# Second chunk's query transposes moved from TensorE to VectorE, with a new load form, in an mLSTM and gelu kernel

## The chip, the cores and the metric

The kernel runs on one core of one Trainium2 chip. The metric is the device time of one execution in microseconds (us). The kernel before takes 467.68 us, the median of three runs (467.54 to 468.31).

The core has a matrix engine (TensorE, PE in the profile), a vector engine (VectorE, DVE), a scalar engine (ScalarE, ACT), GpSimd (POOL), and SyncE (SP), which here only issues DMA transfers. Each engine executes its own instructions in the order in which the program gives them, and waits at an instruction until what that instruction needs is there.

## The reference

An mLSTM cell runs over 768 tokens for 4 batches of 8 heads with 40 numbers each. Per head it keeps a 40 x 40 state C, a vector n and a running maximum m:

```python
m_new = max(f[t] + m, i[t])
C = exp(f[t] + m - m_new) * C + exp(i[t] - m_new) * outer(v[t], k[t])
n = exp(f[t] + m - m_new) * n + exp(i[t] - m_new) * k[t]
y[t] = sigmoid(o[t]) * (C @ q[t]) / max(abs(n @ q[t]), 1)
```

The heads of a token are put side by side (320 numbers), and a feed-forward block follows for the 3072 tokens: `h = x @ w_in` (2048 wide), `g = h * sigmoid(1.702 h)`, `out = g @ w_out` (320 wide). Everything is float32.

## The kernel before, in words

**Chunks.** The 768 tokens are cut into six chunks of 128, numbered w = 0 to 5. A chunk's attention is done in matrix form: scores of its keys and queries, weighted by the gates, plus what the state carries in. Then its 512 tokens (4 batches x 128) go through the feed-forward block. In the main loop (line 888) iteration w does the feed-forward block of chunk w, and interleaves the attention of chunk w + 1 into it. The order is written out by hand: each engine gets its instructions in the order of the Python calls.

**Keys and queries as columns.** The scores need keys and queries with the head's numbers along the partitions, `kT` and `qT`, one tile per batch. There are two ways to them:
- `transposes` (line 372) for chunks 0 and 1. `load` (line 110) brings tokens onto partitions, heads and numbers along the row, in packets of 160 bytes (one head of one token). TensorE transposes two heads at a time into a PSUM tile, four for keys and four for queries per batch, and a copy per tile brings the result to SBUF: keys by ScalarE, queries of chunk 1 by VectorE (line 382).
- `block_transposes` (line 385) for chunks 2 to 5. `load_squares` (line 102) brings rows of four consecutive tokens, in packets of 640 bytes; every row is loaded twice, the second time shifted by 32 numbers and on other partitions. VectorE then transposes blocks of 32 x 32 straight from SBUF to SBUF, one instruction for the keys or the queries of a batch (even n: keys, odd n: queries, n // 2 the batch).

The tile `q_sq` holds the queries in both forms (`q_st` is a view of it). The keys of chunk 1 lie in `k_1`, a view of `t_sb`.

**The weights.** The float32 weights come as raw words and are brought into another form on the chip, in 20 pieces of 512 columns: pieces 0 to 9 are `w_in` (2 and 7 the "rests", the last 64 rows), 10 to 19 are `w_out`. `fetch(n)` issues the load on SyncE; `convert(n)` is two ScalarE instructions and then four on VectorE (lines 256 to 265). The pieces are converted while the feed-forward block of chunk 0 is running, just ahead of their use.

**Iteration 0.** Its first half runs `up` (line 603) for pairs of hidden blocks j = 0 to 7, two pairs per call. A pair takes full matmuls over `w_in_sb` (line 615) and the rest matmuls over 64 rows (line 621): two matmuls of 512 columns, on the two halves of the array. Then ScalarE applies the gelu. Around the calls stand conversions (the list `converted`, line 874), the gates of chunk 1 (j = 3), its value load, and, at j = 4 to 7, `transposes(1, j - 4)`. The pieces are converted in the order 3, 4, then 5 behind the first pair; 6 ahead of pair 2, then 7 and 8; the gates; 9 and 10 ahead of pair 4, then 11 and 12; 13 ahead of pair 6, then 14, 15 and 16.

The second half begins with `columns_turn(1)`, a VectorE transpose of the gate columns. Then `down` (line 744) runs in 16 blocks of four hidden row blocks each; piece 17 is converted ahead of the first, 18 and 19 ahead of the fifth and sixth. Behind certain blocks stand the steps of chunk 1's attention: ScalarE's exponentials of the columns, `scale` on GpSimd, `carry` (the state update, TensorE, line 591), `scores`, `values`.

**Loads around the edit.** SyncE's queue runs in order. After the gate loads of chunk 1 (`load_gates(1)`, line 857), `load(1, "kq")` (line 858) issues three key loads and one query load; the next in the queue are the fetches of pieces 10 to 17. A new DMA also waits until an earlier one that used the same one of eight semaphores has landed.

Of the kernel before, what the change touches and what calls it, by code (L numbers as in the profile page):

```python
# [26 lines left out]
def kernel(  # L27
# [19 lines left out]
    NF = DFF // 128  # L47
    D1 = D + 1
    DP = 64
    W = B * L  # L50
# [44 lines left out]
    def k_of(w):  # L95
        return (k_0, k_1)[w] if w < 2 else k_st[:, 0:BH * D].rearrange("s (h d) -> s h d", d=D)
# [5 lines left out]
    def load_squares(w, what):  # L102
        for dst, src in [((k_sq, k), (q_sq, q))["kq".index(c)] for c in what]:
            x = src[:, :, w * L:(w + 1) * L, :].rearrange("b (p two) (r c) d -> two r (b p) (c d)", two=2, c=4)
            for i in range(2):
                for n in range(2):
                    r, at = slice(i * 64 + n * 32, i * 64 + n * 32 + 32), (1 - n) * 32
                    nc.sync.dma_start(out=dst[r, at:at + BH // 2 * 4 * D].rearrange("r (j x) -> r j x", x=4 * D), in_=x[i])

    def load(w, what, bs=slice(0, B)):  # L110
        hs = slice(bs.start * H, bs.stop * H)
        for c in what:
            if c == "o" and w not in eo:
                eo[w] = ld.tile([L, BH, D], FP, tag="eo", bufs=1, name="eo")
            dst, src = {"k": (k_of(w), k), "q": (q_st, q), "v": (v_st, v), "o": (eo.get(w), o_gate)}[c]
            if w and c in "kv":
                for i, t, r in ((0, slice(0, L), slice(0, L)), (1, slice(0, HL), slice(HL, L)),
                                (1, slice(HL, L), slice(0, HL))):
                    x = src[:, :, w * L + t.start:w * L + t.stop, :].rearrange("b (p two) s d -> two s (b p) d", two=2)
                    nc.sync.dma_start(out=dst[r, i::2, 0:D], in_=x[i])  # L120
                continue
            nc.sync.dma_start(out=dst[:, hs, 0:D],
                              in_=src[bs, :, w * L:(w + 1) * L, :].rearrange("b h s d -> s (b h) d"))
# [226 lines left out]
    def columns_turn(w):  # L350
        c = cols[w] = gate.tile([L, 4 * BH], FP, name="cols")
        V.transpose(out=c[:, 0:3 * BH].rearrange("p (k h) -> p k h", h=BH),
                    in_=raw[w][:, 0:3 * BH].rearrange("p (k t) -> p k t", t=32))
# [16 lines left out]
        A.activation(out=eo[w], in_=eo[w], func=AF.Tanh, scale=0.5)  # L370

    def transposes(w, b, between=None):
        for dst, name in ((kT, "kT"), (qT, "qT")):
            dst[w, b] = work.tile([128, NP, L], FP, tag=name, bufs=4, name=name)
        pt = banks("p_t")
        for x, src in enumerate((k_of(w), q_st)):
            if x and between:
                between()
            for p in range(NP):
                h = b * H + 2 * p  # L380
                T.transpose(pt[:, x, p * L:(p + 1) * L], src[:, h:h + 2, :].rearrange("p a b -> p (a b)"), ident)  # L381
        for x, (dst, copy) in enumerate(((kT, A.copy), (qT, V.tensor_copy if w else A.copy))):
            copy(out=dst[w, b].rearrange("r j t -> r (j t)"), in_=pt[:, x, :])

    def block_transposes(w, n):
        b, (to, name, src) = n // 2, ((kT, "kT", k_sq), (qT, "qT", q_sq))[n % 2]
        at, n = 32 + b * NP * 4 * D, NP * 4 * D
        to[w, b] = work.tile([128, NP, L], FP, tag=name, bufs=4, name=name)
        V.transpose(out=to[w, b].rearrange("d j (r c) -> d j c r", c=4),
                    in_=src[:, at:at + n].rearrange("r (j c d) -> r j c d", c=4, d=D)[:, :, :, 0:32])  # L390
# [212 lines left out]
    def up(w, j, between):  # L603


        x = xT[w].rearrange("p c b t -> p c (b t)")
        ph = {}

        def full(j, first, cs=range(2)):
            for c in cs:  # L610
                for i in range(2):
                    f = 2 * j + i
                    for n in range(2):
                        t = slice(n * W // 2, (n + 1) * W // 2)
                        T.matmul(ph[j][i][:, t], w_in_sb[:, c, f * 128:(f + 1) * 128], x[:, c, t],  # L615
                                 start=(first and c == 0 and n == 0), stop=(not first and c == 1 and n == 1))

        def rest(j, start, stop):
            for i in range(2):
                r = slice(i * 64, i * 64 + 64)  # L620
                T.matmul(ph[j][i], w_in_x[r, j, :], x[r, 2, :], start=start, stop=stop)  # L621

        def gelu(j):
            g = gs[w, j] = gp.tile([128, 2, W], FP, tag="g", name="g")
            for i in range(2):
                A.activation(out=g[:, i, :], in_=ph[j][i], func=AF.Gelu_apprx_sigmoid)

        def open_pair(j):
            ph[j] = [ps_m.tile([128, W], FP, tag="m", name="p_h") for _ in range(2)]

        open_pair(j)
        full(j, True, range(1 if j == 0 else 2))
        if j == 0:
            open_pair(1)
            full(1, True, range(1))
            full(0, True, range(1, 2))
        rest(j, False, True)
        gelu(j)
        between()
        if j:  # L640
            open_pair(j + 1)
        rest(j + 1, j > 0, False)
        full(j + 1, False, range(1 if j == 0 else 0, 2))
        gelu(j + 1)
# [210 lines left out]
            convert_low(0)  # L855
            convert_add(0)
    load_gates(1)
    load(1, "kq")
    open_first(2)
    values(0, 2)  # L860
    open_first(3)
# [26 lines left out]
    for w in range(NW):  # L888
        more = w + 1 < NW
        if w == 0:  # L890
            for j in range(NF // 2):
                if j % 2 == 0:
                    ahead, behind = converted[j // 2]
                    run([(convert, p) for p in ahead] + [(fetch, p) for p in fetched.get(j // 2, ())])
                    up(w, j, lambda: run([(convert, p) for p in behind]))
                if j == 6:
                    load(1, "o")
                if j == 1:
                    wait_for(w_in_sb[:, 1, 512:1024])
                    scale(0, 1)  # L900
                if j < B and j % 2:
                    carry(0, j // 2)
                if j == 3:
                    masks()
                    gates(1)
                if j == 4:
                    load(1, "v")
                    columns_in(1)
                    spread(1)
                if j >= B:  # L910
                    transposes(1, j - B)
        else:
            token_sums(w)
            if more:
                gates(w + 1)
                load(w + 1, "o")
            for j in range(NF // 2):
                up_fast(w, j)
                if w == 1 and j < 4:
                    weight_sums(j)  # L920
                if more and j == 2:
                    load(w + 1, "vk")
                    columns_in(w + 1)
                    spread(w + 1)
                if more and j:
                    for n in ((), (0, 2), (4,), (6, 1), (3,), (5, 7), ())[j - 1]:
                        block_transposes(w + 1, n)
                if more and j == 7:
                    columns_turn(w + 1)
                if 2 <= j < 6:  # L930
                    hidden_difference(w, j - 2)
                if j >= 6:
                    hidden_sums(w, (j - 6,), G)
            gelu_fast(w, NF // 2 - 1)
            hidden_sums(w, (2, 3), V)
        side = attention(w + 1) if more else {}
        if w == 0:
            columns_turn(1)

            blocks = [(lambda b=b, n=n: down(w, b, n)) for n0 in (0, 2) for b in range(B) for n in (n0, n0 + 1)]  # L940
        else:
            blocks = down_fast(w, 0) + down_fast(w, 1)
        for i, block in enumerate(blocks):
            if w == 0 and i in (0, 4, 5):
                convert((17, 18, 19)[max(i - 3, 0)])
            if w + 2 < NW and i == (6 if w == 0 else 0):
                load_gates(w + 2)
            if w + 2 < NW and i == 13:
                load_squares(w + 2, "kq" if w else "k")
            if w == 0 and i == 15:  # L950
                load_squares(w + 2, "q")
            block()
            run(side.get(i, []))
            if w == 0 and i in (11, 13):
                input_sums(slice(0, 4) if i == 11 else slice(4, 8))
# [30 lines left out]
```

## Time and profile before

| | |
|---|---|
| median of three runs | 467.68 us |
| the profiled execution | 468.03 us, its span 466.3 us |
| TensorE busy | 461.4 us, 99% of the span |
| VectorE busy | 341.1 us, 73% |
| ScalarE busy | 189.7 us, 41% |
| GpSimd busy | 156.7 us, 34% |
| chunk 0's feed-forward, first half | 26 to 68.4 us |
| chunk 0's feed-forward, second half | 68.4 to 111.9 us |

A line of the timeline gives start, duration, engine, line of the kernel, operation, output and inputs, the number of merged instructions, and in brackets the idle time ahead of it and what ended it. A line of the groups ends with the total busy time and the mean of one in ns. A line of the DMA issues ends with the median time from issue to landing. The chain of waits is the chain that ended last, followed back from the end; in order of time each line has start, duration and what ran.

### The profile page before, as it was taken

To read this page: it belongs to the slowest core of one execution; us is meant where nothing else is said; L and a number is where in the kernel's file an instruction comes from. 1 tells how busy PE (TensorE), PEld (TensorE's weight loads), DVE (VectorE), ACT (ScalarE), POOL (GpSimd) and SP (SyncE) were. 2 spreads that over 40 slices of the span, in tenths; PEclk is the share of its full clock that TensorE was granted. 3 is DMA by queue.
4 is the path that set the end of the run, shared out by engine and by line. 5 is a ranking of instruction groups with operands and counts; after the bars stand their busy time and mean duration, and the time that the engine had idled before them with its cause. 6 is when DMAs were issued, how large, how long until landed. Compare 5 with 4: busy or idle time off the path is not lost.

```text
span 466.3 us, 12346 instructions
## 1 busy us (share of the span) xinstructions
PE 461.4 (99%) x5063; PEld 387.8 (83%) x5063; DVE 341.1 (73%) x699; ACT 189.7 (41%) x431; POOL 156.7 (34%) x143
## 2 busy tenths in 40 slices
PE   8999999999999999999999999999999999999997
PEld 6867777776778999678999778999878999876997
DVE  5788998689778876688875788887768866545612
ACT  5686778200536600554800453900444820264100
POOL 5101006100798600266800257610148510157100
PEclk9999999999999999999999999999999999999999
DMA  9999969039994035998024989114999405000000
GB/s 169 205 313 151 327 89 216 3 73 189 160 159 106 3 85 129 193 122 147 15 60 115 199 134 148 32 43 115 185 135 117 94 19 139 29 1 0 1 29 30
DMA packets 138393, 52.21 MB, mean 112 GB/s; under 512 B 106976, under 2 KB 134496, under 8 KB 138336
## 3 DMA queue, kind: packets, MB, share of 16 engines
q1 hardware_dynamic: 130288, 49.76, 55.4%
q10 hardware_dynamic: 8048, 1.66, 1.8%
q8 instruction: 40, 0.66, 0.6%
q14 instruction: 17, 0.14, 0.1%
HBM read 43.86 MB, written 7.54 MB: 110 GB/s over the span
## 4 chain that ended last, share of the span: by engine, by line
PE 98%; DVE 1%; issue 0%; ACT 0%; DVEq 0%
PE p_out L803 33%; PE p_h L694 27%; PE p_h L702 8%; PE p_out L749 8%; PE p_h L615 6%; PE p_c L591 3%; PE p_o L498 2%; PE p_s L454 2%; PE p_i L506 2%; PE p_t L381 2%; PE p_h L621 2%; PE p_s L443 1%; PE p_w L410 1%; PE p_idle L197 0%; PE p_o L488 0%; PE p_w L422 0%
## 5 line engine op out<-in xcount | busy, mean ns | idle before, releaser
L740 POOL TENSOR_TENSOR g<-g,parts 128x512 f32<-128x512 f32 x30 | 38.2, 1273 | 190.8 <-DVE parts L732 183.7
L728 ACT COPY parts<-p_h 128x256 f32<-128x256 f32 x40 | 14.9, 374 | 151.5 <-PE p_h L694 147.8
L803 PE MATMUL p_out<-w_out_sb,g 128*128 128x160 f32 x480 | 69.5, 301 | 0.0
L803 PEld LDWEIGHTS p_out<-w_out_sb,g 128*128 128x128 f32 x480 | 66.5, 190 | 0.9
L694 PE MATMUL p_h<-xT,w_in_sb 128*128 128x256 f32 x240 | 66.9, 388 | 0.0
L675 ACT ACTIVATE g<-g 128x512 f32<-128x512 f32 x80 | 50.1, 631 | 39.2 <-DVE g L735 24.5
L694 PEld LDWEIGHTS p_h<-xT,w_in_sb 128*128 128x128 f32 x240 | 43.7, 190 | 18.5 <-issue 6.7
L808 DVE TENSOR_TENSOR o_sb<-o_sb,p_out 128x160 f32<-128x160 f32 x70 | 21.4, 317 | 40.7 <-PE p_out L803 40.1
L803 PE MATMUL p_out<-t_sb,s 128*128 128x160 f32 x320 | 47.1, 300 | 0.0
L731 DVE TENSOR_TENSOR t_x<-p_h,parts 128x256 f32<-128x256 f32 x40 | 16.7, 418 | 38.6 <-PE p_h L702 34.1
L803 PEld LDWEIGHTS p_out<-t_sb,s 128*128 128x128 f32 x320 | 44.4, 190 | 0.2
L694 PE MATMUL p_h<-t_x,s_in 128*128 128x256 f32 x160 | 41.1, 379 | 0.0
L702 PE MATMUL p_h<-xT,w_in_x 64*128 64x512 f32 (+1 forms) x192 | 39.8, 540 | 0.0
L430 ACT ACTIVATE wt<-wt,cols 128x64 f32<-128x64 f32 x160 | 38.8, 333 | 0.1
L749 PE MATMUL p_out<-w_out_sb,g 128*128 128x320 f32 x128 | 35.7, 436 | 0.0
L577 POOL TENSOR_TENSOR vw<-v_st,cols 128x656 f32<-128x656 f32 (+1 forms) x13 | 17.1, 1330 | 51.3 <-ACT cols L363 51.3
L694 PEld LDWEIGHTS p_h<-t_x,s_in 128*128 128x128 f32 x160 | 30.3, 190 | 4.2
L749 PEld LDWEIGHTS p_out<-w_out_sb,g 128*128 128x128 f32 x128 | 23.9, 190 | 9.6
L732 DVE TENSOR_TENSOR parts<-p_h,t_x 128x512 f32<-128x512 f32 x40 | 27.7, 692 | 3.9 <-DVE t_x L731 0.5
L615 PE MATMUL p_h<-xT,w_in_sb 128*128 128x256 f32 x128 | 29.8, 385 | 0.0
L739 ACT COPY g<-p_h 128x512 f32<-128x512 f32 x30 | 17.4, 580 | 30.3 <-PE p_h L702 25.0
L702 PEld LDWEIGHTS p_h<-xT,w_in_x 64*128 64x128 f32 x192 | 16.9, 186 | 14.7 <-issue 13.5
(192 smaller groups left out, 846.9 us busy)
## 6 DMA issues: line engine op xcount, KB each, us to landing
wt<-m_row SPq DMA_DIRECT2D x20, 256.0 KB, 5.0
k_sq<-in_k_dram SPq DMA_DIRECT2D x16, 320.0 KB, 6.2
q_sq<-in_q_dram SPq DMA_DIRECT2D x16, 320.0 KB, 10.6
out_dram<-o_sb SPq DMA_DIRECT2D x24, 160.0 KB, 1.9
eo<-in_o_gate_dram SPq DMA_DIRECT2D x5, 640.0 KB, 8.6
bits<-in_moe_w_in_dram SPq DMA_DIRECT2D x6, 512.0 KB, 10.1
q_sq<-x_row SPq DMA_DIRECT2D x10, 256.0 KB, 2.9
v_st<-in_v_dram SPq DMA_DIRECT2D x14, 160.0 KB, 5.3
```

Source lines behind the costliest of these rows:

```text
L430: A.activation(out=x[:, h, :], in_=x[:, h, :], func=AF.Exp, scale=-1.0, bias=cols[w][:, c * PH + h:c * PH + h + 1])
L577: G.tensor_tensor(out=vw[w, c][:, part * n:(part + 1) * n], in0=v_st[:, hs, :], in1=e, op=OP.mult)
L615: T.matmul(ph[j][i][:, t], w_in_sb[:, c, f * 128:(f + 1) * 128], x[:, c, t], start=(first and c == 0 and n == 0), stop=(not first and c == ...
L675: A.activation(out=gs[w, j][:, i, :], in_=gs[w, j][:, i, :], func=AF.Gelu_apprx_sigmoid)
L694: T.matmul(out, a, x[n], start=start, stop=stop)
L702: T.matmul(row[:, t], w_in_x[r, j, :], rest_x[r, 2, t], start=(not late and h == 0), stop=(late and h == n - 1))
L732: V.tensor_tensor(out=y[:, half_w:3 * half_w].rearrange("p (a t) -> p a t", a=2), in0=flat[:, half_w:3 * half_w].rearrange("p (a t) -> p a ...
L739: A.copy(out=g[:, 0, :], in_=row0)
L740: G.tensor_tensor(out=g0, in0=g0, in1=u, op=OP.add)
L749: T.matmul(po, gs[w, f // 2][:, f % 2, b * L:(b + 1) * L], w_out_sb[:, f, :], start=(f == 0), stop=(f == NF - 1))
L803: T.matmul(po, a(f), b[:, f, :], start=(f == 0), stop=(f == NH - 1))
L808: V.tensor_tensor(out=dst, in0=x, in1=po, op=OP.add)
```

## The change

The queries of chunk 1 are loaded by `load_squares(1, "q")`, four DMAs, ahead of the keys, in place of the one DMA behind them. They are transposed by four block transposes on VectorE: two ahead of the conversions of pair 2 in the first half of iteration 0, two behind `columns_turn(1)`. `transposes` does keys alone for chunk 1, so four TensorE transposes and one VectorE copy per batch are gone. In `up`, the rest matmuls of pairs 4 to 7 are each cut into two of 256 columns.

```diff
     def transposes(w, b, between=None):
-        for dst, name in ((kT, "kT"), (qT, "qT")):
+        both = ((kT, "kT", k_of(w)), (qT, "qT", q_st))[:1 if w else 2]
+        for dst, name, _ in both:
             dst[w, b] = work.tile([128, NP, L], FP, tag=name, bufs=4, name=name)
         pt = banks("p_t")
-        for x, src in enumerate((k_of(w), q_st)):
+        for x, (_, _, src) in enumerate(both):
...
-        for x, (dst, copy) in enumerate(((kT, A.copy), (qT, V.tensor_copy if w else A.copy))):
-            copy(out=dst[w, b].rearrange("r j t -> r (j t)"), in_=pt[:, x, :])
+        for x, (dst, _, _) in enumerate(both):
+            A.copy(out=dst[w, b].rearrange("r j t -> r (j t)"), in_=pt[:, x, :])
...
         def rest(j, start, stop):
-            for i in range(2):
-                r = slice(i * 64, i * 64 + 64)
-                T.matmul(ph[j][i], w_in_x[r, j, :], x[r, 2, :], start=start, stop=stop)
+            n = 2 if j >= NF // 4 else 1
+            for h in range(n):
+                t = slice(h * W // n, (h + 1) * W // n)
+                for i in range(2):
+                    r = slice(i * 64, i * 64 + 64)
+                    T.matmul(ph[j][i][:, t], w_in_x[r, j, :], x[r, 2, t], start=(start and h == 0),
+                             stop=(stop and h == n - 1))
...
     load_gates(1)
-    load(1, "kq")
+    load_squares(1, "q")
+    load(1, "k")
...
             for j in range(NF // 2):
+                if j == 2:
+                    block_transposes(1, 1)
+                    block_transposes(1, 3)
...
             columns_turn(1)
+            block_transposes(1, 5)
+            block_transposes(1, 7)
```

## The prediction

> **What bounds the kernel now.** I read the page's busy shares, then the chain of waits in order of time, then VectorE's timeline and SyncE's queue around the edit.
>
> ```profile
> PE 461.4 (99%) x5063; PEld 387.8 (83%) x5063; DVE 341.1 (73%) x699; ACT 189.7 (41%) x431; POOL 156.7 (34%) x143
> ```
>
> TensorE is the bound, so what is taken off it counts whole unless it then waits. The chain (start, us, what) where the edit acts:
>
> ```profile
> 56.08 1.75 PE p_t L381 x16
> ...
> 66.85 1.75 PE p_t L381 x16
> 68.60 8.62 PE p_out L749 x32
> 77.22 2.01 PE p_c L591 x128
> ```
>
> Each 1.75 us is two of the second chunk's `transposes`, half keys and half queries. TensorE then runs without a gap into `down` and `carry`. VectorE in this stretch, its timeline:
>
> ```profile
> 38.73 0.69 DVE L265 CUSTOM_DVE_ANT_0 w_in_sb<-bits,w_in_sb 128x1024 uint16<-128x1024 uint16 x1
> ...
> 43.01 0.43 DVE L256 TENSOR_SCALAR w_in_x<-w_in_x 128x512 f32<-128x512 f32 x1 [1.23 <-ACT w_in_x L243]
> ...
> 60.87 1.28 DVE L383 COPY qT<-p_t 128x512 f32<-128x512 f32 x2
> ...
> 71.48 1.28 DVE L383 COPY qT<-p_t 128x512 f32<-128x512 f32 x2
> 72.68 0.27 DVE L352 STREAM_TRANSPOSE cols<-raw 128x96 f32<-128x96 f32 x1
> ```
>
> The first line is the end of weight piece 5; piece 6 starts at 39.34. Between there and `columns_turn` (72.68) VectorE has one gap, the bracketed 1.23 us. It is nearly full, and POOL waits behind it for the columns:
>
> ```profile
> 73.37 3.19 POOL L577 TENSOR_TENSOR vw<-v_st,cols 128x656 f32<-128x656 f32 x2 [35.79 <-ACT cols L363]
> ```
>
> The second `scale` ends at 76.56, and the second half of `carry`, which needs it, starts at 77.22 + 1.0 = 78.2: 1.66 us of cover.
>
> SyncE's queue, and times from issue to landing for the small gate load and the first key load:
>
> ```profile
> 27.97 0.32 SPq L92 DMA_DIRECT2D fi<-in_i_gate_dram  x1
> 29.51 8.62 SPq L120 DMA_DIRECT2D t_sb<-in_k_dram  x3
> 38.23 0.61 SPq L122 DMA_DIRECT2D q_sq<-in_q_dram  x1
> ```
>
> ```profile
> fi<-in_i_gate_dram SPq DMA_DIRECT2D x1, 16.0 KB, 9.9
> ```
>
> ```profile
> t_sb<-in_k_dram SPq DMA_DIRECT2D x1, 320.0 KB, 9.9
> ```
>
> The 16 KB gate load needs until 27.97 + 9.9 = 37.9: the weight pieces lie ahead of it. The queries' packets cannot all come sooner.
>
> **What the Trainium skill says.** "DMA: Bandwidth & Descriptors", section "Queues, rings and completion order": on each DMA engine descriptors are consumed in ring order. The trace agrees (37.9 above). The same page, "Why a DMA increments its semaphore by 16 and not by 1": the engines finish independently and only the full count means landed. The trace agrees: of the gate load's 16 arrivals fifteen come by 36.7, the last at 37.9. "VectorE: DVE Perf Modes", "The three transpose paths": VectorE transposes 32x32 blocks only and stays in SBUF, TensorE goes to PSUM. The trace agrees: L381 is followed by copies at L383, L389 by none. "SBUF — State Buffer", "SBUF: two separate sides": VectorE and GpSimd lock a shared port pair. The trace agrees: the two `scale` calls took 1.49 and 1.74 us beside weight conversion, where the one at 36.30 took 1.29.
>
> **The change part by part.**
>
> *Removed from TensorE*: 4 x 4 query transposes, half of 2 x 1.75 us: **-1.75 us** (0.87 from 56.1, 0.87 more from 66.9).
>
> *Halved rests* (pairs 4 to 7): twice the matmuls of half the width. Chunk 4 has this form already (start, us, what):
>
> ```profile
> 331.19 1.93 PE p_h L702 x16
> ```
>
> ```profile
> 115.08 1.92 PE p_h L702 x8
> ```
>
> +0.01 us per two pairs, +0.02 in all.
>
> *VectorE*: four PSUM copies leave. They occupied 60.87 to 62.07 and 71.48 to 72.68, so -1.20 and -1.20. Four block transposes come, which have a row in the later chunks:
>
> ```profile
> L389 DVE STREAM_TRANSPOSE qT<-q_sq 128x512 f32<-128x512 f32 x16 | 17.2, 1117 | 0.0
> ```
>
> Two back to back took 2.06 us at 143.22; 2.1 with the wait. Two stand before piece 6, two after `columns_turn`.
>
> *The load*: one DMA of 4096 packets of 160 B becomes four of 512 packets of 640 B (every row twice, once shifted), ahead of the keys. The later chunks' squares give the rate, over 3 us from 331:
>
> ```profile
> DMA packets 948, 0.59 MB, mean 196 GB/s; under 512 B 28, under 2 KB 948, under 8 KB 948
> ```
>
> 316 packets a us, so 2048 take 6.5 us. (The old query load ran at 2598 in 3 us, 4.7 us.) SyncE issues them in the keys' place from 29.51. The first packets run where the keys' ran, from about 34.4. The engines that are on time end at 40.9; a landing follows its last packet by about 1.2 us (the key load's last packet near 38.2, landing 39.4), so 42.1. The late engine gets to them at 37.9 - 1.2 = 36.7, has done about 83 of its 128 by 40.9 (20 a us), and needs 1.7 to 2.3 us for the other 45: **all landed at about 44.0**, from 41.9 (no engine late) to 46 (slow to its end, or issue blocked by its full ring).
>
> *The new wait.* VectorE comes to `block_transposes(1, 1)` at 39.34 and waits until 44.0: 4.66 us. Queued behind it are pieces 6 to 16, the gates and `columns_turn`. Their delay is 4.66 + 2.1 - 1.23 (the old gap, swallowed) = 5.5 us. What is late next:
> - piece 7, 45.37 + 5.5 = 50.9; its rest matmuls were due at 50.52: TensorE +0.4;
> - piece 9, 53.81 + 5.5 = 59.3; due, with 0.87 saved, at 58.7: 0.6 late;
> - piece 14, 66.78 + 5.5 - 1.2 = 71.1; `down` needs its sixth row block at 66.85 + 6 x 0.54 = 70.1: 1.0 late;
> - `columns_turn`, 72.68 + 5.5 - 2.4 = 75.8. The two `scale` calls start 0.7 later, now beside the block transposes; like L740 at 1.26 to 1.27 us beside L389, they should take 1.29 each: ended at 79.1. The second half of `carry` ends 1.05 later, at 80.15, where it ended at 79.22: **+0.9 us on the old time**.
>
> These are nested, not added: the last contains the others. In general the end moves by (landing - 39.34 - 3.7) us, but by no less than -1.75. I take +1.0 with the halved rests.
>
> *Keys and what follows on SyncE.* Before, the queries landed at 38.23 + 8.1 = 46.3; now the keys come last, at about 46 to 50, against their transposes at 56.1. Pieces 10 to 17, the gate rows and the column loads slide by 2 to 4 us. ACT would take piece 10 at 48.4 and stands idle 2.0 us before the gelu at 51.6; that gelu's banks are wanted by TensorE at 56.8. The column rows landed near 69.5, now by 73.5, ahead of `columns_turn` at 75.8. Nothing on the path; without this cover each late us would cost one.
>
> *After `carry`* VectorE does two block transposes (2.1 us) and piece 17, then the state sums, about 4 us later than before. The score products were done at 90.4 and values begin at 92.4; VectorE had a 4.1 us gap there. I count zero, up to +1 if the gap falls short. From 94.5 on everything starts from TensorE's values, and shifts with it.
>
> **Sum.** On the profiled execution (span 466.3, 1.7 us around it, 468.03): 469.0. The median of the runs, 467.68, lies 0.35 lower: **468.7**.
>
> **The rivals.**
> - *The queries are there in time.* For it: the first packets run at up to 400 a us, and the late engine may take nothing away. Below a landing of 43.0 the kernel gains; at 41.1 the whole 1.75 us is left, 465.9. Against it: 6.5 us from 34.4 alone give 42.1, a gain of 0.9. This is the rival on the other side.
> - *A draw*: landing at 42.1 to 43.9 moves the time by less than 0.94 us, the 0.2% about which a measurement of this kernel cannot tell from no change: 467.7.
> - *Later than I think*: the late engine's ring is full, so the fourth load is issued late, or the keys' issue holds piece 10. With the queries at 46.5 the formula gives +3.5: 471.1. For it: the second key load was held in issue until 37.3. Against it: only the late engine is concerned.
> - *It does not wait at all*, because another query already frees VectorE: excluded, each block transpose reads all 128 partitions, so all four loads.
>
> **How the numbers follow.** VectorE waits and the end is later by over 0.94 us: 0.55, 0.08 of it for the late rival. A draw: 0.28, an early landing of the queries 0.17. The forecast's own range is 467.5 to 470.7; with both signs, 465.9 (all of the gain) to 470.9 (landing at 46.2).
>
> **What would show it.** After: L381 in the second chunk with 16 records instead of 32; VectorE's L389 at about 39 with an idle time of some 4.7 us, ended by a DMA into `q_sq`; TensorE waiting before L621 near 50.5 for `w_in_x`, and before `p_c` near 77 for POOL; from 94 on a constant shift. An idle time before L389 under 2 us, or no TensorE wait before `p_c`, makes the prediction wrong.

## The result, and the profile after

The changed kernel takes 471.94 us, the median of four runs (471.21 to 472.76); the kernel before took 467.81 us beside it. The ratio is 1.0088, with a 95% interval of 1.0066 to 1.0109: slower by about 4.1 us, where 1.0 was predicted, and above the predicted range. The profiled execution took 471.45 us with a span of 469.7 us, 3.4 us more than before. It lies 0.5 us below the median of the changed kernel, and the account from here on is of it.

TensorE's busy time is the same, though 16 transposes are gone. The page's first section, after:

```profile
PE 461.2 (98%) x5063; PEld 387.7 (83%) x5063; DVE 342.7 (73%) x699; ACT 189.2 (40%) x431; POOL 156.6 (33%) x143
```

(The count of records is equal because 16 halves of rests came and 16 transposes went.) VectorE's timeline after; before, piece 6 began at 39.34 behind the line at 38.73, and `columns_turn` stood at 72.68:

```profile
38.70 0.69 DVE L265 CUSTOM_DVE_ANT_0 w_in_sb<-bits,w_in_sb 128x1024 uint16<-128x1024 uint16 x1
46.41 2.06 DVE L390 STREAM_TRANSPOSE qT<-q_sq 128x512 f32<-128x512 f32 x2 [7.02 <-DMA q_sq<-in_q_dram]
...
50.05 0.69 DVE L265 CUSTOM_DVE_ANT_0 w_in_sb<-bits,w_in_sb 128x1024 uint16<-128x1024 uint16 x1
...
77.93 0.27 DVE L352 STREAM_TRANSPOSE cols<-raw 128x96 f32<-128x96 f32 x1
```

VectorE stands still for 7.02 us ahead of the block transposes, and the landing of the query load ends it. The chain of waits, in order of time (start, us, what), goes through this place; before, TensorE alone carried it here:

```profile
35.43 10.86 DMA q_sq<-in_q_dram
...
46.41 2.06 DVE qT L390 x2
...
50.05 0.70 DVE w_in_sb L265
50.75 0.04 issue
50.80 2.76 PE p_h L616 x8
...
72.66 5.28 DMA wt<-m_row
77.94 0.28 DVE cols L352
```

The fourth query load, issued at 35.43, lands at 46.29; piece 6 ends at 50.75, and TensorE has waited for it. The last two lines put the start of `columns_turn` down to another load, the last of the `spread` loads into the weights' tile `wt`. But `columns_turn` doesn't read that tile, and VectorE's timeline shows no idle time ahead of it: the load and VectorE's own work end at the same moment. Run 11, which has no spread loads, tells the two apart. TensorE's timeline, and GpSimd's beside it:

```profile
50.80 2.76 PE L616 MATMUL p_h<-xT,w_in_sb 128*128 128x256 f32 x8 [2.03 <-DVE w_in_sb L265]
53.48 2.87 PE L625 MATMUL p_h<-xT,w_in_x 64*128 64x256 f32 x16
...
79.97 2.39 PE L592 MATMUL p_c<-vw,t_sb 64*64 64x41 f32 x128 [0.56 <-POOL vw L578]
...
114.86 1.03 PE L699 MATMUL p_h<-xT,w_in_sb 128*128 128x256 f32 x4
```

```profile
78.63 2.54 POOL L578 TENSOR_TENSOR vw<-v_st,cols 128x656 f32<-128x656 f32 x2 [41.07 <-ACT cols L363]
```

TensorE loses 2.03 us at piece 6 and 0.56 us at `carry`. Behind piece 6 its granted clock is 0.5 for some 3.4 us (the mean over 51 to 56 us is 0.66), and its matmuls run slower: eight took 2.76 us where 1.99 is usual. The 1.7 us that this adds to its busy time are about what the transposes took off it. The last line is the first matmul of chunk 1's feed-forward block, which I call the mark. Before it was

```profile
111.73 1.03 PE L694 MATMUL p_h<-xT,w_in_sb 128*128 128x256 f32 x4
```

The mark is 3.13 us later, and so is all that follows.

SyncE's queue before (the gate load, at 27.97, is shown above), then after, and the gate load's time to landing after. The lines `m_row<-m_run` write the running maxima out, and the spread loads `wt<-m_row` bring them back in.

```profile
54.40 0.64 SPq L300 DMA_DIRECT2D m_row<-m_run  x1
...
67.05 2.38 SPq L398 DMA_DIRECT2D wt<-m_row  x4
```

```profile
28.76 0.32 SPq L92 DMA_DIRECT2D fi<-in_i_gate_dram  x1
30.39 5.35 SPq L108 DMA_DIRECT2D q_sq<-in_q_dram  x4
37.10 9.51 SPq L120 DMA_DIRECT2D t_sb<-in_k_dram  x3
...
58.70 0.64 SPq L300 DMA_DIRECT2D m_row<-m_run  x1
...
70.86 2.40 SPq L399 DMA_DIRECT2D wt<-m_row  x4
```

```profile
fi<-in_i_gate_dram SPq DMA_DIRECT2D x1, 16.0 KB, 11.1
```

The first weight pieces behind the keys are issued up to 8 us later than before (46.70 where it was 38.93), and everything from `m_row` on about 4 us later.

### The profile page after: what moved, and what is told of

It reads as the page before. It is cut to its first block, busy times and chain, and to the rows that moved or that the text cites. A ratio compares the mean times of both kernels' runs of the same rounds, so it can differ in the third digit from the quotient of the medians.

```text
span 469.7 us, 12348 instructions
## 1 busy us (share of the span) xinstructions
PE 461.2 (98%) x5063; PEld 387.7 (83%) x5063; DVE 342.7 (73%) x699; ACT 189.2 (40%) x431; POOL 156.6 (33%) x143
## 3 DMA queue, kind: packets, MB, share of 16 engines
q10 hardware_dynamic: 8048, 1.66, 1.7%
## 4 chain that ended last, share of the span: by engine, by line
PE 85%; SPq 6%; DMA 6%; DVE 1%; issue 1%; POOL 0%; ACT 0%; DVEq 0%; POOLq 0%
PE p_out L808 33%; PE p_h L699 27%; PE p_h L707 8%; PE p_out L754 6%; SPq L122 3%; DMA bits<-in_moe_w_in_dram 2%; DMA q_sq<-in_q_dram 2%; PE p_o L499 2%; PE p_s L455 2%; PE p_h L616 2%; PE p_i L507 2%; PE p_c L592 2%; SPq L167 1%; DMA wt<-m_row 1%; PE p_h L625 1%
## 5 line engine op out<-in xcount | busy, mean ns | idle before, releaser
L699 PE MATMUL p_h<-xT,w_in_sb 128*128 128x256 f32 x240 | 66.9, 388 | 0.0
L699 PEld LDWEIGHTS p_h<-xT,w_in_sb 128*128 128x128 f32 x240 | 43.7, 190 | 18.5 <-issue 6.7
L707 PE MATMUL p_h<-xT,w_in_x 64*128 64x512 f32 (+1 forms) x192 | 39.8, 540 | 0.0
L616 PE MATMUL p_h<-xT,w_in_sb 128*128 128x256 f32 x128 | 30.8, 392 | 2.1 <-DVE w_in_sb L265 2.0
L616 PEld LDWEIGHTS p_h<-xT,w_in_sb 128*128 128x128 f32 x128 | 23.8, 192 | 8.0 <-issue 2.6
## 6 DMA issues: line engine op xcount, KB each, us to landing
q_sq<-in_q_dram SPq DMA_DIRECT2D x20, 320.0 KB, 10.4
bits<-in_moe_w_in_dram SPq DMA_DIRECT2D x6, 512.0 KB, 10.4
```

Source lines behind the costliest of these rows:

```text
L699: T.matmul(out, a, x[n], start=start, stop=stop)
L707: T.matmul(row[:, t], w_in_x[r, j, :], rest_x[r, 2, t], start=(not late and h == 0), stop=(late and h == n - 1))
```

## The experiments

Two theories were to be told apart. **The wait**: VectorE's wait for the queries delays the weight pieces and `columns_turn`, and through `scale` the second half of `carry`; nothing else matters. **The slide**: the doubled load occupies SyncE and the DMA engines longer, so that what is issued behind it (the gate rows, the rows for `columns_turn`, the four `spread` loads of the running maxima into chunk 1's weights' tile `wt`) is late, wherever VectorE stands. Edits are shown against the changed kernel, or where it says so against the kernel before, which took 467.8 to 468.1 us beside them.

| run | median, us | ratio to before (95%) |
|---|---|---|
| 1 transposes read other data | 472.27 | 1.0079 (1.0053 to 1.0105) |
| 2 new load alone | 469.54 | 1.0040 (1.0018 to 1.0062) |
| 3 halved rests alone | 468.49 | 1.0011 (1.0004 to 1.0017) |
| 4 keys first | 475.48 | 1.0163 (1.0148 to 1.0177) |
| 5 transposes at pair 4 | 473.55 | 1.0117 (1.0102 to 1.0132) |
| 6 old load, other data | 466.57 | 0.9964 (0.9952 to 0.9976) |
| 7 as 5, no spread loads | 468.42 | 1.0005 (0.9994 to 1.0016) |
| 8 load behind the rows | 469.93 | 1.0032 (1.0019 to 1.0045) |
| 9 rows loaded once | 468.07 | 1.0005 (0.9990 to 1.0020) |
| 10 once, behind the keys | 466.14 | 0.9964 (0.9952 to 0.9976) |
| 11 as changed, no spread loads | 472.18 | 1.0087 (1.0070 to 1.0104) |
| 12 whole rests | 471.52 | 1.0078 (1.0056 to 1.0101) |

**1. The wait taken away.** Chunk 1's query transposes read the keys' tile, which is there early.

```diff
-        b, (to, name, src) = n // 2, ((kT, "kT", k_sq), (qT, "qT", q_sq))[n % 2]
+        b, (to, name, src) = n // 2, ((kT, "kT", k_sq), (qT, "qT", k_sq if w == 1 else q_sq))[n % 2]
```

> The changed kernel with everything in its place, but the four block transposes of chunk 1 read the tile of the keys (long since loaded) and not the queries' new load, so nothing waits for that load; chunk 1's queries are then wrong data. Theory W (VectorE's wait for the load sets the end, which moves by landing - 43.0 us, at best by -1.75): no wait at 39, 466.1 us, faster than before by 1.7. Theory S (the slide of keys, pieces and gate rows in SyncE's queue sets the end): the loads are as in the changed kernel, so 471 to 472. Theory V (the VectorE work of the transposes, not the wait, is too much): slower than before still, 468.5 or more.

The wait is gone and the loss stays. ScalarE's timeline before, then this run's timelines of ScalarE and TensorE, and its chain of waits:

```profile
73.69 7.75 ACT L430 ACTIVATE wt<-wt,cols 128x64 f32<-128x64 f32 x32
```

```profile
78.26 7.75 ACT L431 ACTIVATE wt<-wt,cols 128x64 f32<-128x64 f32 x32 [2.24 <-DMA wt<-m_row]
```

```profile
93.88 1.49 PE L499 MATMUL p_o<-v_st,wt 64*64 64x41 f32 x61 [2.86 <-DVE wt L458]
```

```profile
72.58 5.65 DMA wt<-m_row
78.26 2.23 ACT wt L431 x9
...
86.01 0.59 ACT w_out_sb L243
86.62 0.89 DVE w_out_sb L256
```

A spread load lands at 78.2. ScalarE's weights of chunk 1, which began at 73.69 before, begin then; ScalarE's part of piece 18 is queued behind them, VectorE's part behind that, and the multiplication of the scores (L458) behind pieces 18 and 19. TensorE, 1.7 us early at `carry`, waits 2.86 us for it at the values. Then its granted clock is 0.5 for 6.8 us: the 17 us after 95 show

```profile
95.00:112.00 17.00, 17.00 (x248) 12.51 (x244) 12.00 (x25) 0.00 (x0) 0.00 (x0) 0.81 0.34 76
```

with a mean clock (third figure from the end) of 0.81. The sum: -1.71 + 2.86 + half of 6.83 = +4.6; the mark moved by +4.86. Of the run's six executions three, the profiled one among them, have a mean clock of 0.993 or less over the whole span, and took 473.2 to 473.9 us. The three that kept the clock took 469.5 to 471.4 us. So the wait for the queries alone is not the cause: the slide suffices to turn the gain into a loss, and where the clock falls it adds some 2.9 us.

**2. The load alone.** The kernel before with the loads of the new form and order; its TensorE transposes then read rows that lie in the other layout.

```diff
-    load(1, "kq")
+    load_squares(1, "q")
+    load(1, "k")
```

> The kernel before with only the load exchanged: the four square loads ahead of the keys in place of the one query load behind them; TensorE still transposes and VectorE copies, so chunk 1's queries are data in the wrong layout. Theory W: nothing waits for the load before 56 us, 467.8 as before, within 0.5. Theory S: the queue slides as in the changed kernel and the time with it, 470 to 472.

```profile
77.69 7.75 ACT L430 ACTIVATE wt<-wt,cols 128x64 f32<-128x64 f32 x32 [2.07 <-DMA wt<-m_row]
```

```profile
93.31 1.24 PE L498 MATMUL p_o<-v_st,wt 64*64 64x41 f32 x64 [1.01 <-DVE wt L457]
```

The load alone costs 1.5 us, between what the two theories said, with 1.0 us of it at the same place. Here TensorE had gained nothing, and the weights' start at 77.69 was 1.0 us too late: at about 76.7 they would have been in time. Run 1 gives 78.26 - 2.86 + 1.71 = 77.1 for the same limit, counted on the old position of TensorE. Before, they began at 73.69, with 3 us to spare.

**3. The halved rests alone**, in the kernel before (the diff of `rest` above).

> The kernel before with only the halved rests of pairs 4 to 7. Theory W: +0.02 us, no difference (467.8). Theory H (the halved rests cost: the rests of pairs 4 and 5 took 2.87 us in the changed kernel instead of 1.99): +0.9 us or more, 468.7.

+0.5 us, small but above what these runs leave in doubt, where the form accounts for 0.02: sixteen halves take 2.00 us, eight whole ones 1.99. In the profiled execution the mark is 0.57 us earlier than before and the span 0.4 us longer; TensorE stands still for 0.59 us until 169.05, in a later chunk, put down to "issue", where the kernel before has no such gap. What links that to the halves, if anything, is not settled.

**4. Keys first**, the queries' four loads behind them.

```diff
-    load_squares(1, "q")
     load(1, "k")
+    load_squares(1, "q")
```

> The changed kernel with the keys issued ahead of the four square loads. The queries then land about 3 us later than in the changed kernel, near 49. Theory W: VectorE waits 3 us longer and the end moves with it one for one, 475 us. Theory S: the same transfers in all, and piece 10 behind both in either order, so about 472 as the changed kernel.

```profile
49.77 2.00 DVE L390 STREAM_TRANSPOSE qT<-q_sq 128x512 f32<-128x512 f32 x2 [9.97 <-DMA q_sq<-in_q_dram]
```

VectorE goes on 3.36 us later than in the changed kernel, and the mark is at 118.16, 3.30 us later. So the wait counts too, microsecond for microsecond.

**5. The transposes later**, ahead of pair 4 instead of pair 2.

```diff
-                if j == 2:
+                if j == 4:
                     block_transposes(1, 1)
```

> The changed kernel with the first two block transposes ahead of pair 4 (about 51 us) where they stood ahead of pair 2 (39 us); the loads are as in the changed kernel, and the queries have landed by then (46). Theory W (VectorE's wait alone sets the end): the gain of 1.75 us comes out, 466.2. Theory B (a second chain: the gate rows and column loads slide some 4.5 us in SyncE's queue, ScalarE's weights wait for them, and pieces 18 and 19 and the score products behind those): 471 to 473, TensorE waiting about 3 us before the values near 91, as in the run with other data.

The queries are there, at 50.99, without a wait, but the kernel is slower still. `columns_turn` waits 3.14 us for its rows (until 74.89), TensorE 1.90 and 0.44 us in `carry` for the scaled values, and then at the values:

```profile
95.32 1.24 PE L499 MATMUL p_o<-v_st,wt 64*64 64x41 f32 x64 [2.47 <-DVE wt L458]
```

followed by 3.4 us at half clock. Both late loads are of the slide.

**6. Neither.** The old loads in the old order, and the block transposes reading the keys' tile as in run 1.

```diff
-    load_squares(1, "q")
-    load(1, "k")
+    load(1, "kq")
```

> The changed kernel with the old load, one query DMA behind the keys, and the block transposes on the tile of the keys, so both the wait and the slide are gone; only the move of work from TensorE to VectorE is left, with wrong data for chunk 1's queries. Theory B and theory W alike: 466.2, 1.75 us below before. Theory V (the transposes' VectorE time costs by itself): 468 or more.

-1.44 us: the 1.75 us that leave TensorE are worth nearly their whole time when queries and rows are both in time. The block transposes on VectorE, at either place, cost little.

**7. The slide's last part removed.** Run 5 without the spread loads of chunk 1.

```diff
         for c in range(2):
             x = wt[w, c] = work.tile([L, NJ, 2, HL], FP, tag="wt", bufs=2, name="wt")
+            if w == 1:
+                G.memset(x, 0.0)
+                continue
```

> The run with the transposes ahead of pair 4, with the four loads of chunk 1's running maxima into the weights' tile (spread) left out and the tile set to zero by GpSimd; chunk 1's weights are thereby wrong. The column loads before them slide as they did. Theory B: ScalarE no longer waits for those loads, TensorE's wait before the values goes, 466.2 to 467.5 (the column rows still come 2.5 us late for VectorE). If it stays at 471 to 473, the slide acts in another way than through these loads.

5.1 us of run 5's time are gone, though the time is still above the 466.2 to 467.5 expected. ScalarE's weights begin at 76.41, and TensorE waits 0.22 and 0.45 us at `carry` and 0.18 us at the values. The rows for `columns_turn` came 1.0 us sooner too (73.90), which shortens the wait at `carry`; but the wait of 2.47 us at the values and the half clock behind it went with the spread loads. These carry the slide to the end.

**8. The load behind the rows.** Keys in their old place, the squares behind the spread loads, the block transposes in `down`, ahead of the conversions of pieces 18 and 19.

```diff
                     spread(1)
+                    load_squares(1, "q")
...
+            if w == 0 and i in (4, 5):
+                for n in (1, 3) if i == 4 else (5, 7):
+                    block_transposes(1, n)
```

> Keys in their old place, the square loads behind the gate rows and column loads, all four block transposes behind chunk 1's state sums (about 80 us). Neither the early wait nor the slide is there. But the queries land near 82, and VectorE has to do 4.1 us of transposes between there and the values at 91, where it had 4.1 us to spare less what the load costs. Theory B: within 1.5 us of before, 466.5 to 469.5; theory that the early place of the load alone is to blame: 466.2.

`columns_turn` and `carry` are early now (70.22 and 75.35), but the scores wait for the transposes, as TensorE's timeline shows:

```profile
86.84 0.69 PE L455 MATMUL p_s<-qT,kT 40*64 40x64 f32 x32 [1.66 <-DVE qT L390]
```

3.4 us at half clock follow. Of this run's twenty executions thirteen had a mean clock of 0.996 or less, as with such a stretch, and took 469.6 to 471.5 us; the seven that kept the clock took 468.0 to 468.3 us, as the kernel before. So the waits for the transposes take away the gain, and what is lost beyond it comes with the clock. Early rows alone don't suffice where the transposes have no slack.

**9. Half the load, same place.** The rows loaded once; the shifted copy, 8 of every 40 numbers, made by GpSimd ahead of the block transposes.

```diff
-                for n in range(2):
+                for n in range(2 if w > 1 else 1):
...
+    def shift_square():
+        x = q_sq[:, 32:32 + BH // 2 * 4 * D].rearrange("r (k d) -> r k d", d=D)
+        for i in range(2):
+            G.tensor_copy(out=x[i * 64 + 32:i * 64 + 64, :, 0:8], in_=x[i * 64:i * 64 + 32, :, 32:40])
...
                 if j == 2:
+                    shift_square()
                     block_transposes(1, 1)
```

> The changed kernel with the queries' rows loaded once (two DMAs, 1024 packets of 640 B, 0.66 MB) instead of twice; the shifted copy, 8 of every 40 numbers, is made by two GpSimd copies ahead of VectorE's block transposes. Place of the load (ahead of the keys) and of the transposes (ahead of pair 2) stay. If the doubled load is what costs, by its landing and by the slide of SyncE's queue behind it: half the packets at the rates seen land near 42, the copy adds 1 to 2 us, so VectorE goes on at 43 to 44, 2 to 3 us sooner than in the changed kernel; by the landing formula the end is at 0 to +1 us on the time before, 468 to 469, with the load of the m_row issued at 55 to 56 instead of 58.7. If the order of keys and queries alone is what costs, it stays at 471 to 472.

```profile
42.23 2.07 DVE L395 STREAM_TRANSPOSE qT<-q_sq 128x512 f32<-128x512 f32 x2 [3.36 <-POOL q_sq L113]
```

VectorE goes on at 42.23, and the first transfer into `m_row` is issued at 53.67, before its old time. With both parts smaller the loss is gone: the median is that of the kernel before. The gain is not there either; the wait of 3.36 us still pushes `columns_turn` to 73.77, and TensorE waits 0.86 and 0.48 us in `carry`.

**10. Half the load, behind the keys**, as in run 9 with GpSimd's copies, with the transposes of two batches at pair 4, of the other two behind `columns_turn`, and whole rests.

```diff
-    load_squares(1, "q")
     load(1, "k")
+    load_squares(1, "q")
...
                 if j == 2:
+                    shift_square()
+                if j == 4:
                     block_transposes(1, 1)
                     block_transposes(1, 3)
```

> A version meant to beat both: the kernel before with the queries' rows loaded once in rows of four tokens, behind the keys as in the kernel before, the shifted copy by GpSimd at pair 2, block transposes of batches 0 and 1 ahead of pair 4, of 2 and 3 behind the turn of the columns, rests whole. Neither chain of the changed kernel should be left: no VectorE wait for queries, the m_row issued near 54.5, TensorE less than 0.5 us of wait ahead of carry and of the score products. If both chains were all that kept the gain of 1.75 us away: 465.9 to 466.6, at or below the 466.57 of the run with the old load and other data. If something else of the new form costs (GpSimd's copies, the block transposes beside the conversions): 467.5 to 469.

Faster than both kernels: 466.14 us, 0.24 to 0.48% less than before. SyncE's queue and ScalarE's timeline:

```profile
53.73 0.64 SPq L305 DMA_DIRECT2D m_row<-m_run  x1
```

```profile
74.16 7.75 ACT L436 ACTIVATE wt<-wt,cols 128x64 f32<-128x64 f32 x32
```

That transfer is issued 0.7 us earlier than before, the weights don't wait, and TensorE shows no wait of 0.2 us or more between 26.2 and 112 us.

**11. The wait kept, the spread loads gone.** The edit of run 7, made in the changed kernel.

> The changed kernel, transposes ahead of pair 2 as in it, with the second chunk's spread loads of m_row left out and their tile filled with zeros by GpSimd, so the weights of that chunk are wrong and their four loads are missing. The wait for the queries is kept, the late spread loads are gone. If the wait alone carries the loss (the prediction's formula, landing at 46.3): TensorE waits 2 us for piece 6 and 0.5 us ahead of carry, and the time is 471 to 472, as in the changed kernel. If the late m_row chain carries it alone: 467.5 to 468.5, as in the run without spread at pair 4. If either of the two suffices: 471 to 472 here, although the run without spread and without the wait gave 468.4.

```profile
47.30 2.03 DVE L390 STREAM_TRANSPOSE qT<-q_sq 128x512 f32<-128x512 f32 x2 [6.22 <-DMA q_sq<-in_q_dram]
```

The loss of the changed kernel is there in full, although there are no spread loads that could be late. With runs 1, 5 and 7 this makes four cases:

| | spread loads there | spread loads left out |
|---|---|---|
| VectorE waits for queries | 471.94 (changed kernel) | 472.18 (run 11) |
| it does not | 472.27 (run 1), 473.55 (run 5) | 468.42 (run 7) |

Either suffices, and they don't add. Only with both gone is the time that of the kernel before, and with the rest of the slide gone too (run 6) the gain.

**12. Whole rests in the changed kernel.**

```diff
-            n = 2 if j >= NF // 4 else 1
+            n = 1
```

> The changed kernel with whole rests in all pairs. The halving alone cost 0.5 us (interval 0.2 to 0.8) where the form's own duration says 0.02. If that is a cost of the form: 471.3 to 471.6 here. If in the changed kernel it lies under the waits: 471.9, no difference. Less than 471 would say that the halved rests do something else there, like holding TensorE's order at a stall.

No difference can be told from 471.94. One thing in its profile is worth more. TensorE waits as long for piece 6 as in the changed kernel, but keeps its clock (a mean of 1.00 over 51 to 56 us):

```profile
50.74 1.99 PE L616 MATMUL p_h<-xT,w_in_sb 128*128 128x256 f32 x8 [2.05 <-DVE w_in_sb L265]
```

```profile
79.92 2.39 PE L592 MATMUL p_c<-vw,t_sb 64*64 64x41 f32 x128 [0.96 <-POOL vw L578]
```

It only waits longer later, and span and mark (469.7 and 114.86) are those of the changed kernel. The half clock there cost nothing: VectorE's chain set the end. The changed kernel's own executions agree: two with a mean clock of 0.996 took 471.45 and 472.42 us, two with 1.0 took 471.21 and 472.76. At the values (run 1) and the scores (run 8), where TensorE has no further long wait ahead, executions with the fallen clock were 2.9 and 2.3 us slower on the mean.

## Why the prediction was wrong

**Right: the mechanism of the wait and its formula.** The end was said to move by (landing - 43.0) us. Put the start of VectorE's block transposes in place of the landing (0.1 us later, so minus 43.1), and compare the mark's move:

| | start | formula | mark moved |
|---|---|---|---|
| 9 rows loaded once | 42.23 | -0.9 | -0.65 |
| 12 whole rests | 46.34 | +3.2 | +3.13 |
| changed kernel | 46.41 | +3.3 | +3.13 |
| 11 no spread loads | 47.30 | +4.2 | +3.99 |
| 4 keys first | 49.77 | +6.7 | +6.43 |

Five points within 0.3 us. Right too were the block transposes (2.06 us for two, 2.1 said), the two `scale` calls (2.54 us for both, 1.29 each said), the absence of a loss behind `carry` (3.13 there and at the mark), and TensorE's saving (run 6: 1.44 of 1.75 us).

**Wrong: "all landed at about 44.0".** They landed at 46.29, just beyond the far end of the bounds given (41.9 to 46), and this alone turns +1.0 into +3.3. In all seven profiles with the doubled squares in this place they landed at 45.8 to 47.2. The term that failed is the start of the late engine. It was set at 36.7, from the gate load's landing at 37.9; now the gate load was issued at 28.76 instead of 27.97 and took 11.1 instead of 9.9 us, so it landed at 39.8. From there to the queries' landing are 6.5 us, and the late engine's 128 packets at 20 a us are 6.4. The last arrivals of the four loads (41.29, 42.81, 44.67, 46.29) stand 1.5 to 1.9 us apart, which fits 32 packets each at that rate: rate and count were right. Of the 2.3 us, 1.9 are the start. The engines on time were late too: the first of the fourth load's sixteen arrivals came at 43.17, where 42.1 was said for them. Of the 1.9 us, 0.8 are the later issue, which lies within the scatter of all the profiles (27.9 to 29.6). The other 1.2 are the longer way to landing, and that goes with the edit. I had taken what stands ahead in the queue as fixed. It isn't: in the seven profiles with the doubled squares right behind the gate load (the changed kernel, runs 1, 2, 5, 7, 11, 12) it took 11.1 to 12.0 us, in the seven with keys or half the squares there (the kernel before, runs 3, 4, 6, 8, 9, 10) 9.2 to 10.4. The rival "later than I think" had the landing (46.5, 471.1 us) at a chance of 0.08, but for another reason, a full ring that holds the fourth load's issue. That load was held, until 35.43, by an earlier load that landed at 35.41; but with the third load landing only at 44.67, this is not what made it late.

**Wrong: "Nothing on the path" for SyncE.** The slide was put at 2 to 4 us; the first transfer into `m_row` slid by 4.3, and the fetch of piece 10 by 7.8. The cover named was for pieces 10 to 17, the gate rows and the column rows. The list left out the four spread loads at the end of the same run of issues, and what is queued behind them: ScalarE's weights, pieces 18 and 19, the scores' multiplication, the values. Their slack is 3 us (start at 73.69, limit near 77). In the changed kernel this does not show, because the first chain had moved TensorE by 3.1 us and the limit with it, to 80.1; the weights began at 78.94. So it explains none of the measured loss, but all of what the prediction would have got wrong had the queries landed early: the rival "the queries are there in time" at 465.9 could not come about. Run 1 is that case, and took 472.3.

**Wrong in size: the halved rests**, +0.02 said and +0.5 measured alone. In the changed kernel it can't be seen (run 12).

**Partly as said: what would show it.** The 16 transposes, the DMA-ended idle time, the wait ahead of `p_c` and the constant shift are there. The idle time is 7.02 instead of 4.7 us, and so TensorE waits already for piece 6, and not first for piece 7 as said.

What stays open: why loads ahead of the doubled squares land later, and the half microsecond of run 3.

## What to carry to other kernels

Here a load's landing depended on what was queued behind it as well as ahead (the gate load: 11.1 to 12.0 us against 9.2 to 10.4), so a due time read off one landing needs more than its own rate as a margin. When a load in an in-order queue is doubled, list every later issue of that queue down to the last one and give each its slack at the consumer: here two chains, each able to cost 4 us alone (run 11, and run 1 with its fallen clock), hid one another, and mending the visible one brought nothing. And moving data twice to spare an engine a copy is not free: leaving the second 0.66 MB to two GpSimd copies of 0.6 to 0.9 us each took the kernel from 471.9 to 468.1 us (run 9), and to 466.1 with the load in its old place, the transposes later and the rests whole (run 10).

## What was not expected of the hardware

TensorE's granted clock falls to 0.5 after quite short waits, for 3.41 us or twice that. The Trainium skill, "TensorE: Matmul & The Clock Gate", section "HAM oscillation — how this bites in real kernels", warns of idle gaps above about 3.4 us. Here waits of 1.66 (run 8), 2.03 (changed kernel), 2.47 (run 5), 2.86 (run 1) and 2.98 us (run 11) were followed by it, in run 11 at once, and one of 2.05 us (run 12) and one of 1.90 us (run 5, in `carry`) were not. In run 8 one and the same kernel went both ways, thirteen of twenty executions with it and seven without. So gaps well below the page's figure were no protection here. My estimate from these numbers is that a wait of 2 us may cost 3.7, or 6.3 as in run 1 (2.86 + 3.41), if TensorE is what sets the end there.
